# Forward recurrence of an adaLN block with memory attention: causal masks put into the score banks a segment ahead, and small work moved to waits around the out-projection

## The chip, the cores and the metric

The kernel runs on one core of a Trainium2 chip. A core has a matrix engine (TensorE, "PE" in the profile, with its weight loads listed as "PEld"), three engines for elementwise work (VectorE "DVE", ScalarE "ACT", GpSimd "POOL"), and a sync engine ("SP") that here only issues transfers. TensorE writes into PSUM, of which this program uses eight banks; all other operands lie in SBUF. Each engine runs its own instructions in the order of the program, and engines wait for each other through semaphores.

The metric is the time on the device in microseconds for one execution: forward pass and all gradients.

## What is computed

The reference is a transformer block with modulation, run forward and differentiated. The change concerns the attention of the forward pass only: a recurrence over 64 segments of 32 rows, in which 8 memory rows computed by one segment enter the next.

```python
for s in range(n_seg):                         # 2048 rows / 32 = 64 segments
    xs = x[:, s * seg_len:(s + 1) * seg_len, :]
    h = jnp.concatenate([mem, xs], axis=1)     # 8 memory rows + 32 rows = L = 40
    q = jnp.einsum('btd,dhe->bhte', h, Wq)     # 32 heads of 128
    k = jnp.einsum('btd,dhe->bhte', h, Wk)
    v = jnp.einsum('btd,dhe->bhte', h, Wv)
    scores = jnp.einsum('bhqe,bhke->bhqk', q, k) * scale
    scores = jnp.where(mask[None, None], scores, -1000000000.0)
    p = _softmax(scores, axis=-1)
    o = jnp.einsum('bhqk,bhke->bhqe', p, v)
    o = jnp.einsum('bhte,hed->btd', o, Wo)
    mem = o[:, :M, :]                          # M = 8: the next segment waits for this
    outs.append(o[:, M:, :])
# around it:
mod = (_silu(c) @ w_mod).reshape(c.shape[0], 6, 1, -1)   # sa, ca, ga, sb, cb, gb
h = _layernorm(x) * (1 + ca) + sa              # the rows x that the recurrence reads
x = x + ga * A(h)                              # A is the recurrence
x = x + gb * B(layernorm(x) * (1 + cb) + sb)   # B is a gated GLU
```

All of it is then differentiated with respect to eleven inputs; those stages come after the recurrence and are not touched.

## The kernel before

Three heads of 40 rows are packed into one block of 120, so 32 heads make G = 11 groups, handled in three parts of 4, 4 and 3 (`pi` = 0, 1, 2). A segment `s` has a place `s4 = s % 4` in its row tile of 128. The 8 last rows of the four segments of a tile ("tail" columns, `hb`) are projected together, spread over the segments.

The loop of one segment, with the order in which work is given out. The order is pinned, so each engine runs its share exactly in this order:

```python
# psp: 7 rotating PSUM banks (tag "p"); psb: 1 bank for the tail's out-projection
def st_exp(pi):
    st_ps = ps_f32("st_ps")
    for j in range(min(PG, G - pi * PG)):
        g = pi * PG + j
        nc.tensor.matmul(st_ps[:, j, 0:120], lhsT=x120(KT, g), rhs=QT[:, g * 120:g * 120 + 120],
                         start=True, stop=False)
        nc.tensor.matmul(st_ps[:, j, 0:120], lhsT=self.ident[:, :], rhs=maskT[:, :], start=False, stop=True)
    nc.scalar.activation(part3(ET, pi)[:, 0:n, 0:120], st_ps[:, 0:n, 0:120], AF.Exp, scale=cfg.scale)
# den(pi): matmuls of ET with a column of ones into den_ps, a bank of its own (dc_ps)
# pv(pi):  ET x V into or_ps;   recip(a, b): rden = 1 / den_ps
# ost(pi, or_ps, eng): Ost = or_ps * rden ("act": 4 copies with a scale, "dve": one multiply)
# ott(pi): transposes of Ost into tps, copied to OT

proj("k", 0, "dve"); proj("k", 1, "act")
if 1 <= s4 <= 3:
    p1(s // nseg_t + P1_AHEAD, s4)        # LayerNorm steps of a later row tile, see below
proj("q", 0, "dve"); proj("q", 1, "act")
proj("v", 0, "dve")
turns()                                   # transposes of the K and Q rows
proj("v", 1, "dve")
... # copies and small transfers of V
st_exp(0); st_exp(1)
vshift()                                  # moves V rows of the far heads; reads the copy of proj("v", 1)
st_exp(2)
den(0); or0 = pv(0)
if mod_r:
    mod_r.pop()()                         # products of the modulation, 8 matmuls + copy + transfer
if 8 <= s < 8 + 4 * DC:                   # 16 pieces, loaded in s = 8 .. 23, used one segment later
    load, products = self.mod_rest(psp, sb2, s - 8); load(); mod_r.append(products)
den(1); recip(0, 2); or1 = pv(1)
ost(0, or0, "dve"); ost(1, or1, "act")
den(2); or2 = pv(2); recip(2, 3)
ost(2, or2, "dve")
fill(s4, "turn")                          # s4 = 2, 3: transposes of the tail columns' K, Q (turn_ps)
if s4 == 3:
    p1(s // nseg_t + P1_AHEAD, 4)         # transposes of the normalized rows (p1tp), copied by ScalarE (hx)
ott(0); ott(1); ott(2)                    # copied by VectorE, ScalarE, VectorE
self.pop_later(); self.pop_later()        # small transposes and folds of the segment before
at_ps = outproj()                         # 64 matmuls
evac_turned()                             # copies of turn_ps
if s + 1 < NS: tails_in("kq", s + 1)      # GpSimd copies
parts = self.split_pair(sb2, at_ps, "at") # at_hi (ScalarE), then at_lo = at_ps - at_hi (VectorE)
fill(s4, "f1")                            # 16 matmuls of a tail-column projection
ft = self.sum_pair(psp, parts, "at", "p") # fold: the memory rows of the next segment
nc.scalar.activation(hT_next[:, :, 0:M], ft[:, :, 0:M], AF.Copy)
fill(s4, "f2")                            # 16 more
```

The LayerNorm of a row tile goes in steps, which `p1(tile, step)` gives out:

```python
def stats():     # step 1: bn_stats, bn_aggr, + EPS on VectorE, power -1/2 on GpSimd
def scale():     # step 2
    nc.vector.tensor_scalar(xh[:], st["x0"][:], st["mv"][:, 0:1], st["rstd"][:, 0:1], op0=ALU.subtract, op1=ALU.mult)
    nc.vector.tensor_tensor(xh[:], xh[:], ca1_bc[:], op=ALU.mult)
def shift():     # step 3
    nc.vector.tensor_tensor(h1[:], st["xh"][:], sa_bc[:], op=ALU.add)
    nc.gpsimd.dma_start(self.H1ROWS[j * 128:(j + 1) * 128, :], h1[:])
def turn():      # step 4: four transposes, copy hx on ScalarE
```

The fold sums the hi and lo parts:

```python
def sum_pair(self, psp, parts, name, tag):
    ft = psp.tile([128, self.cfg.DC, 32], F32, name=name + "_ft", tag=tag)
    for c in range(self.cfg.DC):
        for i in range(2):
            self.nc.tensor.matmul(ft[:, c, :], lhsT=parts[i][:, (c % 2) * 128:(c % 2) * 128 + 128],
                                  rhs=self.foldhalf[:, c // 2, :], start=(i == 0), stop=(i == 1))
```

At the end of a segment a GpSimd multiply of `Pst` (the transposed probabilities) by `rden` is put off to the start of the next segment.

Of the kernel before, what the change touches and what calls it, by code (L numbers as in the profile page):

```python
# [40 lines left out]
class K:  # L41
# [146 lines left out]
    def mod_rest(self, psp, pool, k):  # L188

        nc, D, DC = self.nc, self.cfg.D, self.cfg.DC  # L190
        sl = slice(2 * D + 128 * k, 2 * D + 128 * k + 128)
        st = {}

        def load():
            st["w"] = pool.tile([128, DC, 128], BF16, name="wmod_r", bufs=1)
            nc.sync.dma_start(st["w"][:], self.io["w_mod"].rearrange("(cc p) n -> p cc n", p=128)[:, :, sl])

        def products():
            ps = psp.tile([128, 128], F32, name="mod_ps", tag="p")
            for n in range(2 * DC):  # L200
                nc.tensor.matmul(ps[0:32, :], lhsT=self.sc_keep[n % 2][:, n // 2, :], rhs=st["w"][:, n // 2, :],
                                 start=(n == 0), stop=(n == 2 * DC - 1))
            row = pool.tile([1, 128], F32, name="modrow", bufs=1)
            nc.scalar.activation(row[:], ps[0:1, :], AF.Copy)
            nc.gpsimd.dma_start(self.MODROW[:, sl], row[:])

        return load, products

# [23 lines left out]
    def sum_pair(self, psp, parts, name, tag):  # L232

        ft = psp.tile([128, self.cfg.DC, 32], F32, name=name + "_ft", tag=tag)
        for c in range(self.cfg.DC):
            for i in range(2):
                self.nc.tensor.matmul(ft[:, c, :], lhsT=parts[i][:, (c % 2) * 128:(c % 2) * 128 + 128],
                                      rhs=self.foldhalf[:, c // 2, :], start=(i == 0), stop=(i == 1))
        return ft

    def col_pass(self, psp, w, hf, lhs, rows, eng):
# [189 lines left out]
    def phase2(self):  # L431
        nc, tc, cfg, io = self.nc, self.tc, self.cfg, self.io
        D, DC, H, E, L, M, T, G, NS = cfg.D, cfg.DC, cfg.H, cfg.E, cfg.L, cfg.M, cfg.T, cfg.G, cfg.NS
        GW = 128
# [10 lines left out]
        with ExitStack() as ctx:  # L445
            wp = ctx.enter_context(tc.tile_pool(name="p2w", bufs=1))
            Wo = wp.tile([128, H, D], BF16, name="Wo")
            maskT = wp.tile([128, 120], BF16, name="maskT128")
            nc.vector.memset(maskT[:], NEG)

            htp = ctx.enter_context(tc.tile_pool(name="p2ht", bufs=3))
            pt = ctx.enter_context(tc.tile_pool(name="p2pt", bufs=1))
            psp = ctx.enter_context(tc.tile_pool(name="p2ps", bufs=7, space=PSUM))
            psb = ctx.enter_context(tc.tile_pool(name="p2psb", bufs=1, space=PSUM))

            def ps_f32(name):
                return psp.tile([128, PG, GW], F32, name=name, tag="p")
# [42 lines left out]
            with tc.tile_pool(name="p0", bufs=1) as p0:  # L500
# [5 lines left out]
                    nc.vector.tensor_copy(dst[:, 96:120].rearrange("p (b r) -> p b r", r=8), v[:, :, 32:L])  # L506
                m_ps = psp.tile([120, 120], F32, name="mask_ps", tag="p")
                nc.tensor.matmul(m_ps[:], lhsT=perm[:], rhs=mcol[:], start=True, stop=True)
                nc.vector.tensor_copy(maskT[0:120, :], m_ps[:])
                p1(0, 0)  # L510
                wmod_v = io["w_mod"].rearrange("(cc p) n -> p cc n", p=128)
                wmod_a = p0.tile([128, DC, 2 * D], BF16, name="wmod", tag="wmod")
# [42 lines left out]
            def x120(t, g):  # L555
                return t[:, g * 120:g * 120 + 128]
# [6 lines left out]
            def turn_half(rows, hf):  # L563
                return self.turn_half(psp, rows, hf)
# [34 lines left out]
            def b_pieces(t):  # L599

                bt = btails[t] = {}
                RBt = dict(RB, v=RBv[t % 2])

                def proj_b(x, hf):
                    hb = hxs[t][1]
                    pass_half(x, hf, lambda c: hb[:, c, :, :].rearrange("p s q -> p (s q)"), RBt[x], ("dve", "act")[hf])
                    if hf == 1 and x != "v":
                        rows_out(RBt[x], DR[x], t * nseg_t, nseg_t)

                def turn_b(x):  # L610
                    bt[x] = btp.tile([128, 8, 128], BF16, name="b_cols" + x)
                    tps = [turn_half(RBt[x], hf) for hf in range(2)]

                    def f():
                        for hf in range(2):
                            self.evac(("act", "dve")[hf], bt[x][:, 4 * hf:4 * hf + 4, :], tps[hf][:])

                    evacs.append(f)

                P = lambda x, hf: (lambda: proj_b(x, hf))  # L620
                T_ = lambda x: (lambda: turn_b(x))
                d = {(s4, "f%d" % (hf + 1)): [P(x, hf)] for s4, x in enumerate("vkq") for hf in range(2)}
                d.update({(s4 + 1, "turn"): [T_(x)] for s4, x in enumerate("vkq") if x != "v"})
                return d
# [15 lines left out]

            norms = []
            mod_r = []
            tail = TailRows(self, sb2, psp, psb, 1, "ao", self.AOB, 2)

            def tails_in(xs, s):
                for x in xs:
# [7 lines left out]
                    nc.gpsimd.dma_start(Vst[96 + 8 * j:104 + 8 * j, 1024:1408], rb[96 + o:104 + o, 384 * j:384 * j + 384])  # L654

            i0 = len(self.traced())
            for s in range(NS):
                s4 = s % nseg_t
                if s4 == 0:
# [24 lines left out]
                        to_heads(eng, XT[x], tp[:], 4 * hf, 4, 32, 0, own=False)  # L684

                def st_exp(pi):
                    st_ps = ps_f32("st_ps")
                    for j in range(min(PG, G - pi * PG)):
                        g = pi * PG + j
                        nc.tensor.matmul(st_ps[:, j, 0:120], lhsT=x120(KT, g), rhs=QT[:, g * 120:g * 120 + 120],  # L690
                                         start=True, stop=False)
                        nc.tensor.matmul(st_ps[:, j, 0:120], lhsT=self.ident[:, :], rhs=maskT[:, :], start=False, stop=True)
                    n = min(PG, G - pi * PG)
                    nc.scalar.activation(part3(ET, pi)[:, 0:n, 0:120], st_ps[:, 0:n, 0:120], AF.Exp, scale=cfg.scale)  # L694

                den_ps = [None]

                def den(pi):
                    if pi == 0:
                        den_ps[0] = psp.tile([128, G], F32, name="dc_ps", tag="p")  # L700
                    n = min(PG, G - pi * PG)
                    for j in range(n):
                        g = pi * PG + j
                        nc.tensor.matmul(den_ps[0][:, g:g + 1], lhsT=ET[:, g * GW:(g + 1) * GW], rhs=self.ones[:, 0:1],
                                         start=True, stop=True)

                def recip(a, b):
                    a, b = a * PG, min(b * PG, G)
                    nc.vector.reciprocal(rden[:, a:b], den_ps[0][0:120, a:b])

                def transposes_part(src, pi, w=GW):
                    ps = ps_b16("tps")
# [12 lines left out]
                                         tile_position=(96, 32 * hl))  # L725
                    nc.vector.tensor_copy(Vst[0:96, 1024:1408], shf[0:96, 0:384])

                def pv(pi):
                    or_ps = ps_f32("or_ps")
                    n = min(PG, G - pi * PG)  # L730
                    for j in range(n):
                        g = pi * PG + j
                        nc.tensor.matmul(or_ps[:, j, :], lhsT=ET[:, g * GW:(g + 1) * GW], rhs=Vst[:, g * GW:(g + 1) * GW],
                                         start=True, stop=True)
                    return or_ps
# [11 lines left out]

                def ott(pi):
                    ps, n = transposes_part(Ost, pi)
                    self.evac("act" if pi == 1 else "dve", part3(OT, pi)[:, 0:n, :], ps)  # L750

                def outproj():
                    ps = psp.tile([128, 256], F32, name="at_ps", tag="p")
# [10 lines left out]
                if s == 0:  # L764
                    for f in firsts["k"]:
                        f()
                if 1 <= s4 <= 3:
                    p1(s // nseg_t + P1_AHEAD, s4)
                proj("q", 0, "dve")
                proj("q", 1, "act")  # L770
                if s == 0:
# [21 lines left out]
                st_exp(2)  # L793
                if s < NS - 1:
                    nc.sync.dma_start(VTr[:], Vst[:, :], transpose=True)
                den(0)
                or0 = pv(0)
                Pst = sb2.tile([128, G, 128], BF16, name="Pst", bufs=1)
                if s < NS - 1:
# [1 line left out]
                else:  # L801
# [1 line left out]
                    nc.gpsimd.dma_start(self.w_up, io["B_w_up"].rearrange("(c p) f -> p c f", p=128))  # L803
                    nc.gpsimd.dma_start(self.w_gate, io["B_w_gate"].rearrange("(c p) f -> p c f", p=128))
                    late_rows()
                if mod_r:
                    mod_r.pop()()
                if 8 <= s < 8 + 4 * DC:
                    load, products = self.mod_rest(psp, sb2, s - 8)
                    load()  # L810
                    mod_r.append(products)
                den(1)
                recip(0, 2)
                or1 = pv(1)
                ost(0, or0, "dve")
                ost(1, or1, "act")
                den(2)
                or2 = pv(2)
                recip(2, 3)
                ost(2, or2, "dve")  # L820
                fill(s4, "turn")
                if s4 == 3:
                    p1(s // nseg_t + P1_AHEAD, 4)
                ott(0)
                ott(1)
                ott(2)
                self.pop_later()
                self.pop_later()
                nc.sync.dma_start(self.OSR[s], gl3(Ost))
                at_ps = outproj()  # L830
                evac_turned()
                if s + 1 < NS:
                    tails_in("kq", s + 1)
                parts = self.split_pair(sb2, at_ps, "at")
# [1041 lines left out]
class TailRows:  # L1876

    def __init__(self, k, pool, psp, psb, n, name, dram_b, npieces=4, tags=""):  # L1880
        self.k, self.pool, self.psp, self.psb, self.n, self.name = k, pool, psp, psb, n, name
        self.dram_b, self.npieces, self.tags = dram_b, npieces, tags
        self.cur = None
        self.pieces = []
        self.whole = None
# [10 lines left out]
    def begin(self, s0, ws):  # L1896
# [8 lines left out]
        def piece(u):  # L1905
            def f():
                if u == 0:
                    st["ps"] = self.psb.tile([128, 512], F32, name=f"{self.name}_tps", tag="b")
                for n in range(u * per, (u + 1) * per):
                    i, h = order[n]  # L1910
                    self.k.col_mm(st["ps"], tiles[i][:, h, :], ws[i][:, h, :], n, len(order))
# [115 lines left out]
```

## Time and profile before

| What | Value |
|---|---|
| Time, median of 3 | 3183.44 us (3178.51 to 3185.88) |
| Profiled execution | 3180.4 us |
| TensorE busy, forward stage (34 to 1014 us) | 947.3 of 980 us, 18125 matmuls |
| VectorE / ScalarE / GpSimd busy there | 596.0 / 476.6 / 634.4 us |
| Granted TensorE clock there | 0.99 |
| Score matmuls `st_ps` (K x Q, mask) | 704 + 704, 218 and 216 ns each |
| Exp `ET<-st_ps` | 192, 566 ns in the median |
| Products of the modulation `mod_ps` (L201) | 128, from 194.0 to 427.7 us |

How to read it: a profile row names the source line, the engine, the operation, the output and input tiles, the shape (for a matmul, rows x columns of the weights, then the moving operand) and a count; in the timeline, the first number is the start in us from the beginning of the span, the second the duration, and a bracket at the end gives how long the engine was idle before and what released it. Matmuls are pipelined, so their durations overlap; the distance between two starts tells what one costs TensorE. The view by stretch of time gives busy time per engine in a window, which is how the forward stage's row was taken.

### The profile page before, as it was taken

How to read it: one execution, taken by the hardware profiler on the slowest of the kernel's cores; microseconds unless marked ns; L12 is line 12 of the kernel's file. 1: busy time of each engine (PE TensorE's matmuls, PEld its weight loads, DVE VectorE, ACT ScalarE, POOL GpSimd, SP SyncE). 2: the span in 40 equal slices, each digit the busy share in tenths (PEclk: the TensorE clock that was granted, in tenths of full speed). 3: DMA queues.
4: the chain of work that ended last, by engine and by line, in shares of the span. 5: the costliest groups of instructions: out<-in, count | busy, mean ns of one | idle time of the engine just before them, and what ended most of it. 6: DMA issues, size and time to landing. Idle time of an engine off the chain costs nothing.

```text
span 3180.4 us, 98869 instructions
## 1 busy us (share of the span) xinstructions
PE 2985.1 (94%) x40069; PEld 1729.6 (54%) x40069; DVE 1579.3 (50%) x3770; ACT 1161.1 (37%) x2829; POOL 1481.1 (47%) x2973
## 2 busy tenths in 40 slices
PE   5999999999998899989999999999999969999999
PEld 3666666666665444445555555555555534445454
DVE  4655666666654777642245455554554521332221
ACT  2454454454454433322244444444444410100011
POOL 3666666666664466521244444444444421233322
PEclk8999999999999899999999999999999989999999
DMA  8788888889888798897599999999999999998886
GB/s 291 206 208 208 202 201 207 198 206 212 198 206 236 182 221 219 209 294 245 171 260 255 265 256 263 268 274 263 263 261 251 261 226 223 231 213 192 204 231 152
DMA packets 958892, 726.12 MB, mean 228 GB/s; under 512 B 656018, under 2 KB 831138, under 8 KB 958308
## 3 DMA queue, kind: packets, MB, share of 16 engines
q1 hardware_dynamic: 827940, 508.77, 71.1%
q0 software_dynamic: 59056, 148.62, 13.9%
q10 hardware_dynamic: 71440, 62.40, 7.8%
q8 instruction: 316, 5.18, 0.7%
q14 instruction: 140, 1.15, 0.1%
HBM read 294.91 MB, written 276.33 MB: 180 GB/s over the span
## 4 chain that ended last, share of the span: by engine, by line
PE 34%; DMA 9%; issue 8%; ACT 3%; POOL 2%; DVE 2%; SPq 1%; ACTq 0%; POOLq 0%; DVEq 0%
PE dh_ps L212 10%; PE gps L1820 5%; PE pass_ps L249 4%; PE g_ps L1509 4%; PE dh_tps L212 2%; DMA rows<-DKR 2%; PE gps5o L1833 2%; PE tps L1424 2%; PE dp_ps L1488 1%; DMA rows<-DQR 1%; PE dp_ps L1496 1%; ACT RAd L61 1%; DMA rows<-OSR 1%; PE dh_ft L318 1%; PE turn_ps L1390 1%
## 5 line engine op out<-in xcount | busy, mean ns | idle before, releaser
L1820 PE MATMUL gps<-rows,hrows 128*128 128x512 bf16 (+2 forms) x2160 | 417.8, 355 | 4.5 <-ACT ot L61 3.1
L1820 PEld LDWEIGHTS <-hrows 128*128 128x128 bf16 x2160 | 211.1, 98 | 209.4 <-issue 5.1
L249 PEld LDWEIGHTS <-hT 128*32 128x32 bf16 x6144 | 158.2, 97 | 161.3 <-issue 1.9
L1538 POOL COPY dOst<-RAd 96x512 bf16<-96x512 bf16 x128 | 78.6, 614 | 356.4 <-DVE RAd L63 345.0
L852 POOL TENSOR_TENSOR Pst<-Pst,rden 120x1408 bf16<-120x1408 bf16 x63 | 161.2, 2559 | 114.7 <-issue 81.5
L1824 POOL DMA_DIRECT2D out_dram<-ot x108 | 81.5, 755 | 232.9 <-DVE ot L63 138.9
L63 DVE CAST ot<-gps 128x512 bf16<-128x512 f32 (+3 forms) x76 | 47.9, 633 | 254.0 <-PE gps L1820 122.5
L309 DVE TENSOR_TENSOR dh_lo<-dh_ps,dh_hi 128x256 bf16<-128x256 f32 x128 | 48.4, 420 | 240.2 <-ACT dh_hi L305 240.2
L1833 PE MATMUL gps5o<-WoT,rows 128*128 128x512 bf16 x600 | 134.3, 387 | 26.6 <-DMA rows<-OSR 26.6
L61 ACT ACTIVATE ot<-gps 128x512 bf16<-128x512 f32 (+3 forms) x75 | 41.2, 549 | 281.4 <-PE gps L1820 128.7
L212 PE MATMUL dh_ps<-WvT,dVT 128*32 128x512 bf16 x2048 | 136.1, 385 | 0.0
L249 PE MATMUL pass_ps<-Wv,hT 128*32 128x512 bf16 x2048 | 133.5, 380 | 0.0
L1498 DVE SCALAR_TENSOR_TENSOR dS<-dp_ps,Pst_l 128x512 bf16<-128x512 f32 (+1 forms) x192 | 112.2, 640 | 35.0 <-PE dp_ps L1496 34.9
L249 PE MATMUL pass_ps<-WoT,dyT 128*32 128x512 bf16 x2048 | 122.9, 382 | 5.2 <-ACT dyT L1597 5.2
L220 PE MATMUL at_ps<-Wo,OT 128*32 128x256 bf16 x4096 | 124.7, 275 | 0.5 <-DVE OT L63 0.2
L249 PE MATMUL pass_ps<-Wk,hT 128*32 128x512 bf16 x2048 | 123.6, 383 | 1.5 <-ACT hT L842 1.1
L63 DVE CAST RA0v<-pass_ps 128x512 bf16<-128x512 f32 x128 | 88.4, 690 | 70.5 <-PE pass_ps L249 68.1
L212 PE MATMUL dh_ps<-WkT,dKT 128*32 128x512 bf16 x2048 | 122.4, 380 | 0.0
L212 PE MATMUL dh_ps<-WqT,dQT 128*32 128x512 bf16 x2048 | 121.9, 379 | 0.0
L249 PE MATMUL pass_ps<-Wq,hT 128*32 128x512 bf16 x2048 | 121.8, 379 | 0.0
L61 ACT ACTIVATE dVT<-g_ps 128x512 bf16<-128x512 f32 (+1 forms) x192 | 108.1, 563 | 36.6 <-PE g_ps L1509 20.5
L694 ACT ACTIVATE ET<-st_ps 128x480 bf16<-128x480 f32 (+1 forms) x192 | 96.2, 537 | 53.7 <-ACT qT L61 37.0
(411 smaller groups left out, 7035.9 us busy)
## 6 DMA issues: line engine op xcount, KB each, us to landing
OSR<-Ost SPq DMA_DIRECT2D x64, 352.0 KB
OT<-OT SPq DMA_DIRECT2D x64, 352.0 KB
VT<-VTr SPq DMA_DIRECT2D x64, 352.0 KB
PS<-Pst SPq DMA_DIRECT2D x64, 352.0 KB
OT_l<-OT SPq DMA_DIRECT2D x64, 352.0 KB
Pst_l<-PS SPq DMA_DIRECT2D x64, 352.0 KB
VT_l<-VT SPq DMA_DIRECT2D x64, 352.0 KB
DKR<-rows_x POOLq DMA_DIRECT2D x64, 352.0 KB, 5.8
```

What stands on the lines that cost most here:

```text
L61: return nc.scalar.activation(out, in_, AF.Copy)
L63: return nc.vector.tensor_copy(out, in_)
L212: self.nc.tensor.matmul(ps[32 * j:32 * j + 32, :], lhsT=lhsT, rhs=w, start=(n < 4), stop=(n >= total - 4), tile_position=(0, 32 * j))
L220: nc.tensor.matmul(ps[32 * j:32 * j + 32, :], lhsT=x[k], rhs=w[k][:, 256 * d:256 * d + 256], start=(n == 0), stop=(n == total - 1), tile_p ...
L249: self.nc.tensor.matmul(ps[32 * j:32 * j + 32, :], lhsT=lhs(c), rhs=rhs, start=(c == 0), stop=(c == DC - 1), tile_position=(0, 32 * j))
L694: nc.scalar.activation(part3(ET, pi)[:, 0:n, 0:120], st_ps[:, 0:n, 0:120], AF.Exp, scale=cfg.scale)
L852: nc.gpsimd.tensor_tensor(Pst[0:120, :, :], Pst[0:120, :, :], rden[:, :].unsqueeze(2).to_broadcast([120, G, 128]), op=ALU.mult)
L1498: nc.vector.scalar_tensor_tensor(out=part3(dS, pi), in0=ps[:, 0:n, :], scalar=cfg.scale, in1=part3(Pst, pi), op0=ALU.mult, op1=ALU.mult)
L1509: nc.tensor.matmul(ps[:, j, :], lhsT=lh[:, g * GW:(g + 1) * GW], rhs=rh[:, g * GW:(g + 1) * GW], start=True, stop=True)
L1820: nc.tensor.matmul(ps[:, 0:ng * E], lhsT=hrows[:, tp_, c * 128:(c + 1) * 128], rhs=rows[:, tp_, 0:ng * E], start=(tp_ == 0), stop=(tp_ == ...
L1824: nc.gpsimd.dma_start(outw[c * 128:(c + 1) * 128, h0:h0 + 3 * (ng - 1) + 1:3, :], ot[:, 0:ng * E].rearrange("p (h e) -> p h e", e=E))
L1833: nc.tensor.matmul(pss[gg][:], lhsT=rows[:, tp_, gg * E:(gg + 1) * E], rhs=dyrows[:, tp_, :], start=(tp_ == order[0]), stop=(tp_ == order[ ...
```

## The change

Five things are done to the segment's loop.

- **Masks ahead.** The score banks become a pool of their own with three banks. For each part one wide matmul (identity x a mask repeated 4 times, 480 or 360 columns) writes the mask into the bank before the scores of the next segment are due, and the score matmuls add to it. The 11 mask matmuls of a segment become 3, given out around the Ost transposes of the segment before. The aim is to have less work ahead of the Exps, and something to do in the wait for Ost.
- **Denominators in the last O bank.** They use the fourth, empty quarter of the bank of `or2` and need no bank of their own. The second and third products with V come before the reciprocal and the last denominators.
- **Modulation products** move from the middle of the chain to the wait for Ost, in other segments (used at s = 4, 7, 8, 12, 16 .. 60), and their copy and transfer go behind the out-projection.
- **LayerNorm steps** 1 to 3 move from between the K and Q projections (s4 = 1, 2, 3) to behind the out-projection (s4 = 0, 1, 2).
- **The fold** takes its four hi matmuls first, then the four lo matmuls. The copies of OT change engines (ScalarE, VectorE, ScalarE), and the eight tail transposes share one bank instead of two.

The rotating pool has 5 banks instead of 7, and the tail's out-projection takes its bank from it too.

```diff
@@ sum_pair
-        for c in range(self.cfg.DC):
-            for i in range(2):
+        for i in range(2):
+            for c in range(self.cfg.DC):
                 self.nc.tensor.matmul(ft[:, c, :], ...,
-                                      ..., start=(i == 0), stop=(i == 1))
+                                      ..., start=(i == 0 and c == 0), stop=(i == 1), skip_group_check=True)
@@ phase2, pools
-            psp = ctx.enter_context(tc.tile_pool(name="p2ps", bufs=7, space=PSUM))
-            psb = ctx.enter_context(tc.tile_pool(name="p2psb", bufs=1, space=PSUM))
+            psp = ctx.enter_context(tc.tile_pool(name="p2ps", bufs=5, space=PSUM))
+            pst = ctx.enter_context(tc.tile_pool(name="p2pst", bufs=3, space=PSUM))
@@ before the loop
+            mod_at = sorted([4 * i + 4 for i in range(4 * DC - 1)] + [7])
-            tail = TailRows(self, sb2, psp, psb, 1, "ao", self.AOB, 2)
+            tail = TailRows(self, sb2, psp, psp, 1, "ao", self.AOB, 2, ptag="p")
+            def mask_mm(pi):
+                n = min(PG, G - pi * PG)
+                ps = masked[pi] = pst.tile([128, PG, GW], F32, name="st_ps", tag="st")
+                nc.tensor.matmul(ps[:, 0:n, 0:120], lhsT=self.ident[:, :], rhs=maskT[:, 0:n, :], start=True, stop=False, ...)
+            for pi in range(NP):
+                mask_mm(pi)
@@ st_exp: st_ps = masked.pop(pi); scores with start=False; no mask matmul
@@ the loop
-                if 1 <= s4 <= 3:
-                    p1(s // nseg_t + P1_AHEAD, s4)
                 proj("q", 0, "dve")
...
-                den(0)
+                or2 = ps_f32("or_ps")
+                den(0, or2)
                 or0 = pv(0)
...
-                if mod_r:
-                    mod_r.pop()()
-                if 8 <= s < 8 + 4 * DC: ...
-                den(1)
-                recip(0, 2)
-                or1 = pv(1)
+                den(1, or2)
+                or1 = pv(1)
+                recip(0, 2, or2)
                 ost(0, or0, "dve")
                 ost(1, or1, "act")
-                den(2)
-                or2 = pv(2)
-                recip(2, 3)
+                pv(2, or2)
+                den(2, or2)
+                recip(2, 3, or2)
                 ost(2, or2, "dve")
+                more = list(range(NP)) if s + 1 < NS else []
+                turned = bool(slots.get((s4, "turn"))) or bool(mod_r)
+                mod_row = mod_r.pop()() if mod_r else None      # the 8 products
+                if s + 1 in mod_at: ...                         # load, append
                 fill(s4, "turn")
                 if s4 == 3:
                     p1(s // nseg_t + P1_AHEAD, 4)
+                    turned = True
+                if more and not turned:
+                    mask_mm(more.pop(0))
+                    mask_mm(more.pop(0))
                 ott(0)
+                if len(more) > 1:
+                    mask_mm(more.pop(0))
                 ott(1)
+                if len(more) > 1:
+                    mask_mm(more.pop(0))
                 ott(2)
+                if more:
+                    mask_mm(more.pop(0))
...
                 at_ps = outproj()
                 evac_turned()
+                if mod_row:
+                    mod_row()                                   # copy and transfer
+                if s4 < 3:
+                    p1(s // nseg_t + P1_AHEAD, s4 + 1)
@@ ott
-                    self.evac("act" if pi == 1 else "dve", part3(OT, pi)[:, 0:n, :], ps)
+                    self.evac("dve" if pi == 1 else "act", part3(OT, pi)[:, 0:n, :], ps)
```

## The prediction

> **What bounds the kernel now.** I read the page from the top: the shares of the engines first, then the slices of the span, then the costliest groups, to find the stage that the change touches.
>
> ```profile
> span 3180.4 us, 98869 instructions
> PE 2985.1 (94%) x40069; PEld 1729.6 (54%) x40069; DVE 1579.3 (50%) x3770; ACT 1161.1 (37%) x2829; POOL 1481.1 (47%) x2973
> PE   5999999999998899989999999999999969999999
> ```
>
> TensorE is busy 94% of the span. The change concerns the forward recurrence alone, 64 segments from 34 to about 1013 us (the first third of the slices). In it 947 of 980 us count as PE busy (busy time by stretch), but that overstates: the 120-column matmul "lasts" 216 ns while the next starts about 53 ns later, so a wait shorter than some 0.15 us is not seen. I therefore read the starts of the matmuls in the timeline, segment by segment. An undisturbed segment takes 14.7 to 14.9 us, of which about 13 us is matmul issue. The rest is short waits on the chain scores, Exp, denominator, product with V, scaled copy Ost, its transpose, out-projection, fold, next segment's memory. From the timeline of segment 29, with lines of other engines between them left out:
>
> ```profile
> 500.62 0.23 PE L690 MATMUL st_ps<-qT,kT 128*128 128x120 bf16 x1
> ...
> 501.30 1.59 ACT L694 ACTIVATE ET<-st_ps 128x480 bf16<-128x480 f32 x3 [0.76 <-ACT qT L61]
> ...
> 501.56 0.34 PE L723 MATMUL sh_ps<-RA0v,ident 32*32 32x384 bf16 x3
> ...
> 503.00 0.69 DVE L745 TENSOR_TENSOR Ost<-or_ps,rden 120x512 bf16<-120x512 f32 x1
> ...
> 503.75 1.09 PE L716 MATMUL tps<-ident,Ost 128*128 128x128 bf16 x11 [0.29 <-DVE Ost L745]
> 503.88 0.56 DVE L745 TENSOR_TENSOR Ost<-or_ps,rden 120x384 bf16<-120x384 f32 x1
> ...
> 504.88 1.93 PE L220 MATMUL at_ps<-Wo,OT 128*32 128x256 bf16 x64
> ...
> 507.61 0.19 PE L237 MATMUL at_ft<-foldsel,at_hi 128*128 128x32 bf16 x1
> 507.82 0.19 PE L237 MATMUL at_ft<-foldsel,at_lo 128*128 128x32 bf16 x1
> ```
>
> The reader is to see the waits: the Ost transposes end on VectorE (after the second Ost), and the fold waits 0.21 us between its first hi part and its first lo part. Two disturbances come on top. In segment 9 the modulation products stand inside the chain:
>
> ```profile
> 194.05 0.62 PE L201 MATMUL mod_ps<-wmod_r,sc_keep 128*32 128x128 bf16 x8
> 194.71 0.27 ACT L204 ACTIVATE modrow<-mod_ps 1x128 f32<-1x128 f32 x1 [0.34 <-PE mod_ps L201]
> 195.27 1.14 ACT L742 ACTIVATE Ost<-or_ps,rden 120x128 bf16<-120x128 f32 x4 [0.30 <-PE or_ps L733]
> ```
>
> And in segment 30 (the next after 29) a LayerNorm step of VectorE starts while GpSimd multiplies Pst, runs five times its least, and delays the q transposes:
>
> ```profile
> 510.35 2.54 POOL L852 TENSOR_TENSOR Pst<-Pst,rden 120x1408 bf16<-120x1408 bf16 x1 [1.54 <-issue]
> 510.67 2.50 DVE L401 TENSOR_SCALAR xh<-x,mv,rstd 128x512 f32<-128x512 bf16 x1
> ```
>
> The view of the tile xh gives least, median and longest duration (ns) of that instruction:
>
> ```profile
> L401 DVE TENSOR_SCALAR xh<-x,mv,rstd x16: 537/1906/2804, 7.5 to 869.8; 128x512 f32<-128x512 bf16 x16
> ```
>
> **What the Trainium skill says.** "TensorE: Matmul & The Clock Gate", section "Wait — 56ns, not 53.3ns?", gives N / 2.4 GHz + 2.5 ns from start to start of warm matmuls, and never under about 25 ns. The trace agrees: 53 ns at 120 columns, 25 to 26 ns at the 32 columns of the fold. For the new masks I estimate from that page 480 columns = 202 ns and 360 = 152 ns; no run has shown them yet. "SBUF — State Buffer", section "Who interferes with whom", says that a VectorE tensor_scalar in a two-port mode, or one with two SBUF inputs, and a GpSimd instruction block each other for the whole instruction. The trace agrees: xh lasts 537 ns at least and 2804 ns at most. "PSUM — Partial Sum Buffer", section "Engine vs sequencer instructions", calls the queues of ScalarE and VectorE strictly first in, first out; the lines of segment 9 show what follows, the modrow copy holding the Ost copies behind it.
>
> **The change, part by part.**
>
> *Modulation products.* The stretch from the first denominator to the first Ost transpose takes 1.59 us in a plain segment and 2.25 in segments 9 to 24, which carry the products (with s mod 4 = 3: 1.81 and 2.46). So each costs 0.66 us: 8 x 0.056 = 0.45 of issue, and the copy in ScalarE's queue. The new place is after the last denominator, where TensorE waits for the first Ost anyway, in segments with s mod 4 = 0 that have no transposes of tail columns there (and once, s = 7). The copy goes behind the out-projection, where ScalarE idles. Gain 16 x 0.66 = 10.6 us.
>
> *LayerNorm steps.* The 8 K transposes take 0.46 us to the first Q transpose when nothing disturbs. Summed over the segments, what is above 0.46 is 5.0 us at s mod 4 = 2 (scale), 2.1 at 3 (shift), and 0.2 in one V pass: 7 us. Behind the out-projection VectorE has no work from about 505.5 (the at_rb copies) to 507.34 (at_lo), 1.8 us. Scale needs 0.54 + 0.69 = 1.23 at its shortest, statistics 0.69 + 0.18 + 0.15 = 1.0, shift 0.69. They fit if GpSimd, which then issues two small transfers and starts the tail copies only at about 506.8, doesn't lock them. Gain 7 us.
>
> *Fold order.* Four hi matmuls now fit in the 0.21 us wait for at_lo, and only four lo's follow: 3 x 0.025 = 0.075 us less, 63 times: 4.8 us.
>
> *Masks.* Eleven mask matmuls of 53 ns (0.58 us) leave the score block, and three wide ones come back after the last denominator: 2 x 0.20 + 0.15 = 0.55. TensorE's work is the same; only waits can be won. With time 0 at the first score (500.62 above), and durations of the trace: the first Exp starts at 0.44, not 0.68. But vshift reads what VectorE copies from 0.19 to 0.88, so it stays at 0.94 and TensorE idles 0.5 us before it; the third score group, 0.15 us shorter, ends at 1.37, and the third Exp starts at 1.58, not 1.80. The first reciprocal moves from 2.14 to 1.98, Ost 0 ends at 2.91 (3.08 before), the second Ost at 3.66 (3.83), the first transpose at 2.97 (3.13). From there:
> - s mod 4 = 1: two masks lie in the wait before it, free. Transposes to 3.54, the last three at 3.72 to 3.89, one mask, two small transposes: out-projection at 4.15, before 4.27.
> - s mod 4 = 0 (products in the wait): 0.22 + 0.20 + 0.22 + 0.20 + 0.17 + 0.15 from 2.97, then 0.35 of tail fold: 4.48, before 4.41.
> - s mod 4 = 2 (tail transposes in the wait): the same without the fold: 4.19, before 4.21.
> - s mod 4 = 3: ScalarE copies hx between its Ost and the first OT, which is now its own: OT lands at 4.39, out-projection 4.45, before 4.31.
> Sum over four segments: -0.12 + 0.07 - 0.02 + 0.14 = +0.07, so 16 x 0.07 = 1 us lost.
>
> *Banks.* The rotating PSUM pool falls from 7 + 1 banks to 5, with 3 for scores. In the order of the changed program, the banks of the Ost transposes are those of the shift, of the V pass and of the first O products, released before they are asked for by the times above. The tightest is the second V pass, which waits for VectorE's copy of the first: it ends at -1.07 and is wanted at -0.98. I count nothing.
>
> **Sum:** -10.6 - 7 - 4.8 + 1 = -21.4 us. All later stages are bound by TensorE and unchanged in code, so they should only start earlier: 3183.4 - 21.4 = 3162.
>
> **Rivals.** (1) Five banks are too few: TensorE would wait for copies at each pass. For it: the 0.09 us margin; against: copies of 0.6 to 0.69 us against 0.86 us per half pass. At 0.2 us per segment it takes back 13 us: 3175. (2) Masks fill no wait but lengthen TensorE's own stretch, and moving the first OT to ScalarE delays the out-projection: for it, my sums leave TensorE nearly full there; at 0.2 us in three of four segments, 10 us back: 3172. (3) VectorE's steps collide with GpSimd at the new place and delay at_lo, straight on the recurrence: up to 0.5 us in 42 segments (14 row tiles x 3 steps) in the worst case, all of the gain. (4) The earlier Exp pays in full, 0.24 us in each segment, if vshift or Ost is less binding than I read: 15 us more, 3147.
>
> **Range and chances.** The products and the fold are read off repeated, equal stretches; I trust them to 2 us. The uncertain terms are 0.15 us per segment, 10 us, in the score stretch, and 4 us in LayerNorm; the three times before span 7 us. Range 3148 to 3176. Two per cent would be 64 us, one whole microsecond per segment; neither a gain nor a loss of that size is in sight.
>
> **What would show each step.** Equal den-to-transpose stretches in segments 9 to 24 and the rest; xh near 0.54 us and no wait of turn_ps for RA q; four at_hi starts ahead of the first at_lo; 192 mask matmuls 0.2 us apart from the next start; Exp 0.24 us earlier but vshift unmoved at 0.94; out-projection at 4.15 to 4.48 after the first score. New waits of pass_ps for copies, or at_lo later than 0.42 us after at_hi starts, would make it wrong.

## The result and the profile after

The changed kernel takes 3166.09 us (median of 4, 3163.81 to 3167.03), against 3183.27 us for the kernel before: a ratio of 0.9947, 95% interval 0.9929 to 0.9964. That is 17.2 us less where 21.4 were predicted, and inside the range.

First the page of the changed kernel: span, busy shares, TensorE by slices.

```profile
span 3162.0 us, 97694 instructions
PE 2978.5 (94%) x39481; PEld 1708.9 (54%) x39557; DVE 1532.8 (48%) x3706; ACT 1186.0 (38%) x2893; POOL 1476.0 (47%) x2973
PE   6999999999997999989899999999999969999999
```

The shares look as before; TensorE's 94% says nothing about the change. The stage has to be measured. The last matmul of the recurrence's last out-projection starts at 992.5 us, before at 1012.2: the forward stage gives 19.6 us. What follows that start took 2169.5 us in this execution and 2168.2 before.

Segment 29 again (s mod 4 = 1), from the timeline of the changed kernel, with lines left out; its first score is at 484.86:

```profile
484.86 0.59 PE L710 MATMUL st_ps<-qT,kT 128*128 128x120 bf16 x8
...
485.33 1.63 ACT L712 ACTIVATE ET<-st_ps 128x480 bf16<-128x480 f32 x3 [0.55 <-ACT qT L61]
485.38 0.74 PE L735 MATMUL sh_ps<-RA0v,ident 32*32 32x384 bf16 x3
486.06 0.33 PE L710 MATMUL st_ps<-qT,kT 128*128 128x120 bf16 x3
...
487.07 0.69 DVE L757 TENSOR_TENSOR Ost<-or_ps,rden 120x512 bf16<-120x512 f32 x1
...
487.33 0.57 PE L659 MATMUL st_ps<-maskT,ident 128*128 128x480 bf16 x2
...
487.82 1.02 PE L728 MATMUL tps<-ident,Ost 128*128 128x128 bf16 x11
...
489.04 1.93 PE L224 MATMUL at_ps<-Wo,OT 128*32 128x256 bf16 x64
...
489.36 0.54 DVE L406 TENSOR_SCALAR xh<-x,mv,rstd 128x512 f32<-128x512 bf16 x1
...
491.77 0.27 PE L241 MATMUL at_ft<-foldsel,at_hi 128*128 128x32 bf16 x4
...
491.98 0.27 PE L241 MATMUL at_ft<-foldsel,at_lo 128*128 128x32 bf16 x4
```

What to see: the first Exp starts 0.47 us after the first score (0.68 before), but the shift (sh_ps) now lasts 0.74 us instead of 0.34. Its first matmul starts early, because it reads columns copied long before; the next ones wait for the same copy of V as ever, and the third scores stand behind it. Two masks fill the wait for Ost. The LayerNorm step runs beside the out-projection at its shortest. The four hi matmuls of the fold fit in the wait for the lo part.

Segment 28 (s mod 4 = 0) carries the modulation products in that wait:

```profile
472.22 0.22 PE L716 MATMUL or_ps<-ones,ET 128*128 128x1 bf16 x3
472.37 0.62 PE L201 MATMUL mod_ps<-wmod_r,sc_keep 128*32 128x128 bf16 x8
...
472.92 0.40 PE L728 MATMUL tps<-ident,Ost 128*128 128x128 bf16 x4
473.15 0.37 PE L659 MATMUL st_ps<-maskT,ident 128*128 128x480 bf16 x1
```

The products occupy TensorE from 472.37 to the transposes at 472.92: 0.55 us, not the 0.45 of eight issues (in the kernel before, the next matmul came 0.55 us after the first product as well). That is the step of the prediction that was off; it comes back below.

The view of the tile xh (least, median, longest ns) answers the one before:

```profile
L406 DVE TENSOR_SCALAR xh<-x,mv,rstd x16: 536/536/593, 5.9 to 845.4; 128x512 f32<-128x512 bf16 x16
```

For the accounting I took the starts of the matmuls from the timeline of every segment and summed the stretches over segments 1 to 62:

| Stretch (us, 62 segments) | before | after | difference | predicted |
|---|---|---|---|---|
| K transposes to Q transposes (LayerNorm steps) | 35.5 | 28.4 | -7.1 | -7 (with one V pass) |
| first score to out-projection (products, masks, Ost) | 278.0 | 273.0 | -5.0 | -10.6 + 1 = -9.6 |
| out-projection to the next K pass (fold) | 252.2 | 246.6 | -5.6 | -4.8 |
| the rest | 368.8 | 368.7 | -0.1 | 0 |
| segment 0, with the first loads | 31.3 | 29.8 | -1.5 | not counted |

Segment 0 was 29.4 to 31.3 us long in the profiles of this study with no relation to the edits, so its 1.5 us is not the change's. The 62 segments alone give 17.8 us.

### The profile page after: what moved, and what is told of

Its sections match the earlier page's. It is cut to its first block, busy times and chain, and to the rows that moved or that the text cites. A ratio compares the mean times of both kernels' runs of the same rounds, so it can differ in the third digit from the quotient of the medians.

```text
span 3162.0 us, 97694 instructions
## 1 busy us (share of the span) xinstructions
PE 2978.5 (94%) x39481; PEld 1708.9 (54%) x39557; DVE 1532.8 (48%) x3706; ACT 1186.0 (38%) x2893; POOL 1476.0 (47%) x2973
## 4 chain that ended last, share of the span: by engine, by line
PE 33%; issue 10%; DMA 8%; POOL 3%; ACT 2%; DVE 1%; SPq 1%; ACTq 0%; POOLq 0%; DVEq 0%
PE dh_ps L216 9%; PE pass_ps L254 4%; PE gps5o L1859 4%; PE gps L1846 4%; PE g_ps L1535 3%; DMA rows<-DKR 2%; PE dh_tps L216 2%; PE tps L1450 2%; DMA dOst<-RBd 1%; PE dp_ps L1514 1%; PE dp_ps L1522 1%; DMA Kst<-KST 1%; ACT RAd L61 1%; DMA out_dram<-ot 1%; POOL out_dram L1850 1%
## 5 line engine op out<-in xcount | busy, mean ns | idle before, releaser
L63 DVE CAST dKT<-g_ps 128x512 bf16<-128x512 f32 (+1 forms) x192 | 112.2, 641 | 1.3
```

What stands on the lines that cost most here:

```text
L63: return nc.vector.tensor_copy(out, in_)
```

## The experiments

All times are medians beside runs of the kernel before on the same chip; ratios are to those. Since the code behind the recurrence is the same everywhere, and took 2157 to 2181 us from one profiled execution to another, I add for each kernel the start of the last matmul of the last out-projection in its profile (1012.2 before, 992.5 for the changed kernel), and the length of segments 1 to 62 (934.5 and 916.7 us), which leaves out segment 0. A segment that nothing disturbs agrees between profiles within about 0.02 us; what makes the sums differ otherwise is named.

| Run | Median us | Ratio, 95% interval | Last out-projection matmul at | Segments 1 to 62 |
|---|---|---|---|---|
| e1_ln | 3173.01 | 0.9964 (0.9951 to 0.9977) | 1003.5 | 926.6 |
| e2_mod | 3170.32 | 0.9965 (0.9950 to 0.9979) | 1001.0 | 923.7 |
| e3_fold | 3177.63 | 0.9985 (0.9973 to 0.9998) | 1007.5 | 931.5 |
| e4_nomask | 3166.17 | 0.9948 (0.9932 to 0.9965) | 996.3 | 920.5 |
| e5_ot | 3162.92 | 0.9937 (0.9913 to 0.9961) | 992.3 | 916.7 |
| e6_early | 3148.89 | 0.9885 (0.9858 to 0.9912) | 980.1 | 903.8 |
| e7_banks | 3197.40 | 1.0048 (1.0031 to 1.0065) | 1032.2 | 956.5 |
| e9_early_ot | 3142.34 | 0.9869 (0.9844 to 0.9894) | 976.8 | 901.4 |
| e10_modfull | 3165.30 | 0.9953 (0.9934 to 0.9972) | 991.4 | 915.4 |
| e11_best | 3140.43 | 0.9867 (0.9845 to 0.9888) | 972.3 | 896.9 |
| e12_order | 3150.16 | 0.9906 (0.9886 to 0.9926) | 984.0 | 908.4 |
| e13_nomask_best | 3158.01 | 0.9916 (0.9890 to 0.9942) | 985.4 | 909.8 |

### One part of the change at a time

**LayerNorm steps alone**, on the kernel before:

```diff
-                if 1 <= s4 <= 3:
-                    p1(s // nseg_t + P1_AHEAD, s4)
...
                 evac_turned()
+                if s4 < 3:
+                    p1(s // nseg_t + P1_AHEAD, s4 + 1)
```

> The kernel before with the LayerNorm steps alone moved behind the out-projection. Theory: the steps cost 7 us where they stood, by a VectorE instruction locked out by GpSimd; 8 K transposes then take 0.46 us in every segment, xh stays near 0.54 us, and the time falls by 6 to 8 us (about 3176). Rival: GpSimd's work meets them at the new place too and at_lo comes late: no gain, 3183.

The stretch from K to Q transposes falls from 35.5 to 28.4 us, 0.46 us in every segment: the 7.1 us of the theory. The median is 10 us below that of before, the interval reaches from 7.3 to 15.6 us less, and segments 1 to 62 are 7.9 us shorter. GpSimd doesn't meet the steps at the new place: xh takes 535 to 547 ns there.

**Modulation products alone**, on the kernel before (the new list of segments, products after the last Ost is given out, the copy behind the out-projection):

```diff
-                if mod_r:
-                    mod_r.pop()()
                 den(1)
...
                 ost(2, or2, "dve")
+                mod_row = mod_r.pop()() if mod_r else None
...
                 evac_turned()
+                if mod_row:
+                    mod_row()
```

> The kernel before with the modulation products alone moved to the wait for Ost (their copy behind the out-projection). Theory: 16 segments lose 0.66 us each, the new place costs nothing: 10 to 11 us less, about 3173. Rival: the products, 0.55 us with the change of tile shape, push the Ost transposes back by 0.1 us or more in the 15 segments with s mod 4 = 0, and two to three us of it are lost: 3175 to 3176.

From the first denominator to the out-projection, the 62 segments lose 10.4 us (181.9 to 171.4); the first score to the out-projection as a whole loses 10.8. One of the sixteen sets of products wins nothing: at s = 7, a segment with s mod 4 = 3, the out-projection comes 0.69 us later than in the others of its place, as much as the products cost before. About 0.6 us of rare waits that went away cover that. In segments with s mod 4 = 0 the first Ost transpose does come 0.19 us later (1.78 after the denominators, 1.59 without products), but the out-projection doesn't: there the last transposes wait for the second Ost, and absorb it. So in these 15 segments the rival's delay exists and costs nothing.

Where the products cost 0.66 us at the old place can be read in segment 9 of the kernel before:

```profile
193.73 0.38 PE L733 MATMUL or_ps<-Vst,ET 128*128 128x128 bf16 x4
194.05 0.62 PE L201 MATMUL mod_ps<-wmod_r,sc_keep 128*32 128x128 bf16 x8
194.60 0.25 PE L704 MATMUL dc_ps<-ones,ET 128*128 128x1 bf16 x4
```

From the last of these four matmuls of or_ps to the next denominators (dc_ps) it takes 0.70 us in the 16 segments with products and 0.055 without: TensorE alone accounts for 0.65 of the 0.66.

**Fold order alone**, on the kernel before:

```diff
-        for c in range(self.cfg.DC):
-            for i in range(2):
+        for i in range(2):
+            for c in range(self.cfg.DC):
...
-                                      ..., start=(i == 0), stop=(i == 1))
+                                      ..., start=(i == 0 and c == 0), stop=(i == 1), skip_group_check=True)
```

> The kernel before with the order of the fold alone changed. Theory: 0.076 us less from the first fold matmul to the second tail projection, 63 times: 4.8 us, about 3178.5. Rival: something else ends the stretch (the copy of the memory rows) and nothing changes.

The stretch from out-projection to the next K pass falls from 252.2 to 247.5 us: 4.7, where 4.8 was predicted. In this profile the LayerNorm steps, still at the old place, collided a little more (37.4 us from K to Q transposes, 35.5 before; 36.2 in e2_mod and 37.1 in e7_banks). An edit elsewhere can shift VectorE's steps against GpSimd's; that this is the reason was not tested.

### The score stretch

**Masks back beside the scores**, on the changed kernel, everything else kept:

```diff
-                    st_ps = masked.pop(pi)
+                    st_ps = pst.tile([128, PG, GW], F32, name="st_ps", tag="st")
...
-                        nc.tensor.matmul(st_ps[:, j, 0:120], ..., start=False, stop=True, ...)
+                        nc.tensor.matmul(st_ps[:, j, 0:120], ..., start=True, stop=False)
+                        nc.tensor.matmul(st_ps[:, j, 0:120], lhsT=self.ident[:, :], rhs=maskT[:, 0, :], start=False, stop=True)
```

> The changed kernel with the masks back beside the scores (11 of 120 columns per segment, none ahead), everything else of the change kept. Theory: the masks ahead earn nothing, because the shift waits for VectorE's copy of V and TensorE has the same work elsewhere: the time stays within 3 us of the changed kernel, 3163 to 3169; by place in the tile, the out-projection moves by +0.10 (s mod 4 = 1), -0.2 (0), -0.07 (2), +0.19 us (3). Rival: the earlier Exp pays in full, so undoing it costs 0.24 us in each segment: 3181.

The medians are equal, 3166.17 and 3166.09. Segments 1 to 62 are 3.8 us longer, so "nothing" was not quite right; by place in the tile a segment changes by +0.17 (s mod 4 = 1), -0.08 (0), -0.02 (2) and +0.17 us (3). In the changed kernel the largest-looking part of the change earns a few microseconds at most. The rival's full 0.24 us per segment is refuted here.

**Third scores ahead of the shift**, all masks still a segment ahead:

```diff
-                vshift()
                 st_exp(2)
+                vshift()
```

> The changed kernel with the third score group ahead of the shift, all three masks still behind the Ost transposes of the segment before. Theory: the third Exp at 1.41 us instead of 1.63 moves Ost by 0.09 us only (VectorE's copies set it), and the other half of the gain of the earlier run was the third mask's 0.15 us: so 5 to 7 us below the changed kernel, about 3160. Rival: the order gives the whole gain, about 3151.

and **the third mask too**, into the hole before the shift:

```diff
                 st_exp(1)
-                vshift()
+                mask_mm(2)
                 st_exp(2)
+                vshift()
...
-                more = list(range(NP)) if s + 1 < NS else []
+                more = list(range(2)) if s + 1 < NS else []
```

> The changed kernel with the third score group ahead of the shift, and its mask put in there too instead of behind the Ost transposes of the segment before. Theory: TensorE idles 0.4 us before the shift (it waits for VectorE's copy of V), so both are free there; the third Exp starts at 1.41 us after the first score instead of 1.63, Ost ends 0.1 us earlier, one mask of 0.15 us leaves the full stretch: the out-projection 0.2 to 0.24 us earlier in each segment, 13 to 15 us in all, about 3152. Rival: VectorE's chain (V copy, copy of the shift, reciprocal, Ost) sets the end and only the mask's 0.15 us is won where TensorE was full: 5 to 7 us, about 3160.

In segment 29 of the second run, from its timeline, with the first score at 479.71:

```profile
480.14 0.32 PE L659 MATMUL st_ps<-maskT,ident 128*128 128x360 bf16 x1
480.18 1.40 ACT L712 ACTIVATE ET<-st_ps 128x480 bf16<-128x480 f32 x3 [0.55 <-ACT qT L61]
480.30 0.32 PE L710 MATMUL st_ps<-qT,kT 128*128 128x120 bf16 x3
480.55 0.43 PE L735 MATMUL sh_ps<-RA0v,ident 32*32 32x384 bf16 x3
...
482.55 1.02 PE L728 MATMUL tps<-ident,Ost 128*128 128x128 bf16 x11
...
483.77 0.45 PEld L224 LDWEIGHTS <-OT 128*32 128x32 bf16 x20 [0.26 <-ACT OT L61]
```

The three Exps now follow each other without a hole (1.40 us, 1.63 in the changed kernel, 1.59 before), the mask and the third scores cost nothing, and the first Ost transpose comes 2.84 us after the first score instead of 2.96. The order alone shortens segments 1 to 62 by 8.3 us and the mask by 4.6 more, 12.9 together. So the shift was what held the third Exp back, and the theory of the order alone gave it too little (5 to 7 us): the third Exp gains what it said (1.39 us after the first score, 1.63 in the changed kernel), but the first Ost transpose moves by 0.12 us, not 0.09. The last line names the next limit: the out-projection waits 0.26 us for ScalarE's copy of OT.

**Copies of OT on the engines of before**, on the changed kernel and on the run above:

```diff
-                    self.evac("dve" if pi == 1 else "act", part3(OT, pi)[:, 0:n, :], ps)
+                    self.evac("act" if pi == 1 else "dve", part3(OT, pi)[:, 0:n, :], ps)
```

> The changed kernel with the copies of OT on the engines of before (VectorE, ScalarE, VectorE). Theory: only segments with s mod 4 = 3 notice, where ScalarE's copy hx stands ahead of the first OT; there the out-projection starts 0.1 us earlier, 14 times: 1 to 2 us less, about 3164.5. Rival: VectorE, behind its second Ost, becomes the limit in the other segments too: 3 to 6 us more.

> The third scores ahead of the shift as in the run before it, and the copies of OT on VectorE, ScalarE, VectorE. Theory: the two gains add: 1 to 2 us below that run, about 3150. Rival: with Ost earlier the copies of OT by VectorE end the wait in every segment: 2 to 5 us above it.

On the changed kernel it is worth nothing that can be measured (916.7 us for segments 1 to 62 in both; 0.06 us less with s mod 4 = 3, where 0.1 was expected, and 0.02 more with 0). On the run above it shortens segments 1 to 62 by 2.4 us: a segment is 0.16 us shorter with s mod 4 = 1, 0.21 with 3, unchanged with 2, and 0.17 longer with 0. The same edit is idle while TensorE is full and counts once it waits.

**Products on the whole array**, on the changed kernel:

```diff
-            k = const.tile([128, DC, 32], BF16, ...)          # weights of the products
+            k = self.keep_pool.tile([128, DC, 128], BF16, ...)
...
-                nc.tensor.matmul(ps[0:32, :], lhsT=self.sc_keep[n % 2][:, n // 2, :], ...)
+                nc.tensor.matmul(ps[:, :], lhsT=self.sc_keep[n % 2][:, n // 2, :], ...)
```

To find room, the tile hx has two buffers instead of three and the weights lie in a pool of the forward stage.

> The changed kernel with the weights of the modulation products widened from 32 to 128 columns (same result in every row, row 0 used), so that these eight matmuls use the whole array as their neighbours do. Theory: each change between the 32-column tile and the whole array costs TensorE about 0.1 us; without the two changes around the products the first Ost transpose comes at 2.96 instead of 3.09 us after the first score in segments with s mod 4 = 0, the out-projection 0.13 us earlier, 2 us in 15 segments. Rival: the products wait for their weights or their bank, whatever their shape: 3.09 as before.

Segment 28, from its timeline, first score at 469.20:

```profile
471.60 0.21 PE L717 MATMUL or_ps<-ones,ET 128*128 128x1 bf16 x3
471.68 0.61 PE L201 MATMUL mod_ps<-wmod_r,sc_keep 128*128 128x128 bf16 x8
472.17 0.40 PE L729 MATMUL tps<-ident,Ost 128*128 128x128 bf16 x4
```

With four times as many columns the eight products start 0.08 us after the first of the last three denominators (0.15 with the narrow tile), and the transposes 0.49 us after the first product (0.55). The first Ost transpose is at 2.96, the out-projection at 4.50 instead of 4.63: as expected, to 0.01. The segments together win 1.3 us of the 2, because those with s mod 4 = 2 and 3 are about 0.02 us longer here, for a reason that stays open. At s = 7, where transposes of tail columns follow the products and wait for nothing, these start 0.44 us after the first product instead of 0.55. "TensorEngine Tiling (Array Packing)", section "Key Properties", says that changing the tiling mode drains TensorE; it gives no time. Here a pair of changes costs 0.13 us where the first transpose then meets its own wait, and 0.07 + 0.11 us at s = 7, where it doesn't.

**Fewer banks**, on the kernel before:

```diff
-            psp = ctx.enter_context(tc.tile_pool(name="p2ps", bufs=7, space=PSUM))
+            psp = ctx.enter_context(tc.tile_pool(name="p2ps", bufs=5, space=PSUM))
```

> The kernel before with 5 rotating PSUM banks instead of 7 and nothing else changed. Theory: the copies release the banks in time, at most 1 us: 3182 to 3185. Rival: TensorE waits for banks at the passes, 0.2 us per segment: 3196.

My theory fell: 15.7 us more between the medians, 22.0 in segments 1 to 62, of which 20.2 lie between the first score and the out-projection. The time is that of the rival, but not its place: the passes take what they took before. This is harsher than the change, since the scores take their banks from the same five. The loss is in segments with s mod 4 = 2 and 3, where the tail transposes take two banks more (the out-projection 0.62 and 0.75 us later after the first score); those with 0 and 1 are unchanged. From the waits of TensorE's weight loads and of TensorE in this run:

```profile
PEld L258 <- DVE Ost L745: 5.3, 22, 0.2
PE at_ps L220 <- ACT OT L61: 6.9, 29, 0.3
```

The first line is transposes (L258) that read nothing of Ost, waiting until VectorE, making Ost, has read the bank that they need; the second is the out-projection waiting for an OT that comes late for it. The kernel before has no line like the first, and one wait like the second. So banks can bind. The changed kernel shows no such wait of transposes, and each pass takes what it took before (1.73 us for K, 1.73 for Q). It asks for fewer banks: denominators in the last O bank, one tile for the eight tail transposes, scores in banks of their own. Which of these are needed was not tested.

### The best version, and what the masks are worth in it

Third scores and mask ahead of the shift, products on the whole array, and OT copies by VectorE, ScalarE, VectorE except with s mod 4 = 0:

```diff
-                    self.evac("dve" if pi == 1 else "act", part3(OT, pi)[:, 0:n, :], ps)
+                    self.evac("dve" if (pi == 1) == (s4 == 0) else "act", part3(OT, pi)[:, 0:n, :], ps)
```

> All that helped: third scores and their mask ahead of the shift, products on the whole array, copies of OT on VectorE, ScalarE, VectorE except where s mod 4 = 0, which keeps ScalarE, VectorE, ScalarE. Theory: 0.16 us in each segment with s mod 4 = 0 from the engines and 0.13 from the shape, 4 us below the run with the first two: about 3138. Rival: with s mod 4 = 0 the out-projection waits for something else (its bank) and the gain is under 1 us: 3142.

3140.43 us, ratio 0.9867 to the kernel before: 41 us less, more than twice the change. A segment with s mod 4 = 0 takes 14.60 us, 14.90 in the run before it: 0.30, expected 0.29. Segments 1 to 62 give 4.5 us, expected 4. The median is not to be told from that of e9_early_ot.

The same version with the masks back beside the scores:

> The best version so far with the masks back beside the scores (11 of 120 columns per segment, none ahead). What do masks ahead earn once the scores don't wait for the shift? Theory: the third Exp at 1.62 us instead of 1.39, the first Ost transpose 0.2 us later, of which 0 to 0.24 us reaches the out-projection by place in the tile, about 0.1 in the mean: the forward stage 5 to 8 us longer, about 3147. Rival: masks ahead still earn nothing, since TensorE's work is the same: 3140.

3158.01 us, and segments 1 to 62 are 12.9 us longer, more than the 5 to 8 expected: 0.24, 0.30, 0.12 and 0.18 us per segment (s mod 4 = 0 to 3). The masks ahead are worth 3.8 us of these segments in the changed kernel and 12.9 here.

## Why the prediction was right, and where it was off

- **Modulation products, 10.6 us:** the sum came true (e2_mod, 10.4), but its parts were misread. The prediction put the 0.66 us of a segment down to 0.45 of issue and to the copy in ScalarE's queue, and said that in segment 9 this copy holds the Ost copies behind it. Its own lines show otherwise: the copy ends at 194.98, and ScalarE then idles 0.30 us until TensorE has written or_ps. TensorE's own 0.65 us is nearly all of it (e2_mod above). And the set at s = 7 wins nothing (0.69 us late in e2_mod, 0.74 in the changed kernel), so that "16 x 0.66" was 15 x 0.66 and some luck with rare waits.
- **LayerNorm steps, 7 us:** right in mechanism and size, shown by e1_ln and by xh at 536 ns in the changed kernel.
- **Fold order, 4.8 us:** right, shown by e3_fold. The 5.6 of the changed kernel hold in addition rare waits with s mod 4 = 1.
- **Masks, "16 x 0.07 = 1 us lost":** the mechanism was right (nothing is won, and TensorE is nearly full), the size was not. The first Ost transpose was put at 2.97 us after the first score; with s mod 4 = 1 it is at 2.96. The out-projection was put at 4.15, 4.48, 4.19 and 4.45 us (s mod 4 = 1, 0, 2, 3) and is at 4.18, 4.63, 4.29 and 4.52. These are 0.03, 0.15, 0.10 and 0.07 too late, 0.35 in four segments, 5.4 us in 62. This term was 1 us of loss and measured 6.4. Rare waits in this stretch fell from 1.1 to 0.3 us, with the 0.74 of s = 7 among them, which leaves the 5.0 us of the table.
- The step that was mis-sized is the sum "0.22 + 0.20 + 0.22 + 0.20 + 0.17 + 0.15 from 2.97". With s mod 4 = 0 its start was wrong: the first Ost transpose comes at 3.10, because I counted eight issues for the products, 0.45 us, as if TensorE changed from the narrow tile to the whole array for nothing, and they take 0.55. e10_modfull shows 0.13 of the 0.15. With 2 the start is right, 2.96, and the end is wrong: the out-projection starts 0.15 us after the last small transpose, against 0.056 for one issue. The same 0.15 stands at this place in the kernel before; that it is again the change to a 32-column tile was not tested. With 1 this error is there too, and luck hides it: the last mask starts at 3.82 where 3.89 was put. With 3 the out-projection waits for ScalarE's OT behind hx, as predicted, 0.07 later; e5_ot takes that wait away and wins 0.06.
- **Banks, nothing counted:** right for the changed kernel by the length of its passes. The reason I gave (copies are done in time) is not general: e7_banks shows the opposite for the old layout.
- **Rivals.** (1) is refuted for the change. (2) is half of the answer: TensorE was full, and the first OT on ScalarE binds with s mod 4 = 3, by 0.06 us. (3) is refuted: at_lo starts 0.42 us after at_hi as before. (4), the Exp paying in full, failed for the reason given, the shift; with that out of the way, e13_nomask_best shows 0.12 to 0.30 us per segment.
- The total: 21.4 predicted; 19.6 less in the forward stage of the profiles, 1.5 of it in segment 0 and not the change's, 17.8 in segments 1 to 62; 17.2 between the medians. That the last two agree so well is chance: the stages behind the recurrence, whose code is the same, vary by more than the difference.

## What to carry to other kernels

A change that moves work into a wait is worth what the wait can hold and no more: measure the wait from the starts of the matmuls, segment by segment, and count the cost of changing the tile shape as work too. Before moving work off the front of a chain, look for what stands in order behind it and waits for someone else: one line moved ahead of the shift gave 8.3 us, and in the version with this and three smaller edits the masks ahead were worth 12.9 us instead of 3.8. And an edit that measures as nothing may count once the limit ahead of it is gone, so try it again after each step.

## What was not expected of the hardware

- A matmul that goes from the whole array to a tile of 32 columns, or back, costs TensorE about 0.07 to 0.1 us in these profiles: eight products started 0.15 us after the first of the last three denominators on the narrow tile and 0.08 on the whole array, and the transposes behind them followed 0.55 and 0.44 us after the first product where they waited for nothing (s = 7). Using a quarter of the array's columns was the dearer way.
- The wide masks cost what the estimate said: 0.20 us from the start of a 480-column matmul to the next, where four masks of 53 ns took 0.21.
- The same edit of engines for one copy moved a segment by -0.21, -0.16, 0 and +0.17 us, depending on its place in the row tile.
